# Fewer, larger transfers of V, wo and w_up, and reader-less matmuls placed anew, in a decode layer on one core

## The chip, the cores and the metric

The kernel runs on one core of a Trainium2 chip. The metric is the device time of one execution in microseconds; the time before is the median of three runs, 188.31 us (188.06 to 188.40).

## The reference

One decode step (one token, batch 2) of a transformer layer whose two halves are modulated by a condition c. Model width D = 640, 32 heads of width 192, the last W = 1024 rows of a cache of 4096, and a feed-forward part of width 1536. Everything is bfloat16. Cut to what matters:

```python
mod = (silu(c) @ w_mod).reshape(B, 6, 1, D)            # sa, ca, ga, sb, cb, gb
h = layernorm(x) * (1 + ca) + sa
q = (h @ wq) as [b, 32, 1, 192]
k, v = k_cache[:, :, -1024:], v_cache[:, :, -1024:]
o = softmax(q @ k.T * 192 ** -0.5) @ v                 # for each b and head
x = x + ga * (o as [b, 1, 6144] @ wo)
h = layernorm(x) * (1 + cb) + sb
out = x + gb * ((gelu(h @ w_gate) * (h @ w_up)) @ w_down)
```

## The kernel before

Each operation is appended to a list of its engine in program order, and the lists are emitted as they stand, with semaphore waits worked out from what each operation reads and writes. So every engine works strictly in the order in which the functions are called. All transfers are issued by SyncE, one after the other, through one queue; a transfer that has to wait for its buffer holds up those behind it on SyncE.

The stages are:

- The modulation w_mod and the projection wq are loaded, then the caches. A cache item is a transfer of one or two tiles. A tile is 64 positions of each partition (a head has four partitions), so that four tiles make up the window of one batch row. There are six places for tiles: four in `ring`, and two in `r1`, once wq is used up. `items` lists the transfers in order with their slot and their semaphore, and `load_kv(n)` issues them up to the n-th.
- Scores (`d_mul` L465, `p_reduce` L476, `d_rows` L483): VectorE multiplies half a tile of K with the query, TensorE sums it with 12 matmuls against an identity matrix, VectorE adds up the rest. The softmax of both batch rows follows.
- Weighted sum (`d_mask` L511, `p_pv` L523): for each tile VectorE spreads the weights over a mask and TensorE runs 32 matmuls over the tile of V, called PV here. `normalize` (L536, L540) and `p_sel` (L548, 8 matmuls each batch row) bring the heads together. Four copies and three VectorE transposes (L599, the tiles `oT`, 16 each) make the left operand of the projection.
- Projection wo (L630): 48 tiles, four matmuls of 32 columns each a tile, one TensorE operation for each transfer of wo, all in one accumulator. wo lies in `r1`, so that its transfers wait for the last PV of batch row 0.
- Second layer norm (a chain of VectorE operations, from L636 to the transpose L358), then `ffn_gu` (L648) for w_gate and w_up, 20 matmuls in all for each. Gelu on ScalarE (L655), product `geglu` (L662), transpose (L358), and the `down` projection (L671) of 12 tiles in three transfers. The product with the gate and the residual sum (L678, L680) and the store close the kernel. w_gate, w_up and w_down lie in slots of `ring`, and their transfers wait for the first two PV of batch row 1.

Between these stand matmuls without a reader: `warm(n, bk)` (L454) runs n matmuls of an identity matrix with the query into a PSUM bank that nobody reads, and `filler(n)` runs 4 n of them. They occupy TensorE for a while where it would stand idle.

```python
def filler(n=1):
    warm(n * ND, BK_W)          # ND = 4
```

Of the kernel before, what the change touches and what calls it, by code (L numbers as in the profile page):

```python
# [103 lines left out]
def bass_adaLN_cond__sliding_block_cached__geglu_ffn__decode_kernel(  # L104
# [49 lines left out]
    NS = 4  # L154
    SL = J * Dh
    WQ_SPLIT = [5]
    assert sum(WQ_SPLIT) == KT
    WO_SPLIT = [16, 16, 12, 4]
    OT_SPLIT = [16, 16, 16]
    assert sum(WO_SPLIT) == NT and sum(OT_SPLIT) == NT  # L160
    WU_SPLIT = [3, 2]
    assert sum(WU_SPLIT) == KT
    WD_SPLIT = [6, 4, 2]
    assert sum(WD_SPLIT) == FT
    ND = 4

    WO_WARM = [0, 8, 0, 9]
    WU_WARM = [3, 5]
    WD_WARM = [5, 0, 0]

    es = ExitStack()
    with es:
        S = _Sched(nc, es)
# [21 lines left out]
        def tile_f(slot, n=1):  # L195
            if slot < NS:
                return ring_f[:, slot * SL:(slot + n) * SL]
            return r1[:, (slot - NS) * SL:(slot - NS + n) * SL]
# [60 lines left out]
        def bank(k):  # L259
            return ("bank", k)  # L260
# [4 lines left out]
        sem_wq = [S.sem("d_wq%d" % i) for i in range(len(WQ_SPLIT))]  # L265
        sem_wo = [S.sem("d_wo%d" % i) for i in range(len(WO_SPLIT))]
        sem_wg = S.sem("d_wg")
        sem_wu = [S.sem("d_wu%d" % i) for i in range(len(WU_SPLIT))]
        sem_wd = [S.sem("d_wd%d" % i) for i in range(len(WD_SPLIT))]
        sem_ring = [S.sem("d_ring%d" % i) for i in range(4)]  # L270
        sem_out = S.sem("d_out")

        def k_dma(dst, src):
            return lambda e: e.dma_start(dst, src)  # L274
# [48 lines left out]
        def ring_keys(slot):  # L323
            return [half_key(slot, 0), half_key(slot, 1)]
# [9 lines left out]


        items = [("k", 0, 0, 2, 0, 0), ("k", 0, 2, 2, 2, 1), ("k", 1, 0, 2, NS, 2), ("k", 1, 2, 2, 0, 0), ("v", 0, 0, 2, 2, 1),
                 ("v", 0, 2, 2, NS, 2), ("v", 1, 0, 2, 0, 0), ("v", 1, 2, 1, 2, 1), ("v", 1, 3, 1, 3, 3)]
        place = {(kind, b, t0 + i): slot + i for kind, b, t0, nt, slot, _ in items for i in range(nt)}
        assert NTL == 4 and len(place) == 4 * NTL

# [3 lines left out]
        def load_kv(upto, deps=()):  # L344
            while keep["kv"] < upto:
                kind, b, t0, nt, slot, sm = items[keep["kv"]]
                cache = A_v_cache if kind == "v" else A_k_cache
                S.dma("sp", k_dma(tile_f(slot, nt),
                                  cache[b, :, K0:Sk, :].rearrange("h (q r) d -> h q r d", q=QP)[:, :, J * t0:J * (t0 + nt), :].rearrange("h q r d -> h q (r d)")),
                      sem_ring[sm], writes=[k for i in range(nt) for k in ring_keys(slot + i)], deps=deps, name="ld_%s%d_%d" % (kind, b, t0))  # L350
                keep["kv"] += 1
# [98 lines left out]
        def warm(n, bk):  # L450
            def f(e):
                last = None
                for _ in range(n):
                    last = e.matmul(ps[:, bk, 0:2 * Dh], lhsT=ident_b[:, :], rhs=qbc[:, :, :].rearrange("p b d -> p (b d)"),  # L454
                                    start=True, stop=True)
                return last
            if n:
                S.op("pe", f, reads=["ident_b", "qbc"], writes=[bank(bk)], name="warm")

        def filler(n=1):  # L460
            warm(n * ND, BK_W)
# [48 lines left out]
        def d_mask(b, t):  # L510
            S.op("dve", lambda e: e.tensor_tensor(out=Em[:, t % 2, :, :], in0=E_sb[:, b, J * t:J * (t + 1)].unsqueeze(2).broadcast_to([P, J, H]),  # L511
                                                  in1=M32b[:, :].unsqueeze(1).broadcast_to([P, J, H]), op=ALU.mult),
                 reads=[("E", b), "M32b"], writes=[("Em", t % 2)], name="mask%d_%d" % (b, t))

        def p_pv(b, t):
            vs = slot_of("v", b, t)
            n = J // 2

            def f(e):
                last = None  # L520
                for jp in range(n):
                    r = 2 * SQ * (jp % 2)
                    last = e.matmul(ps[r:r + 2 * H, BK_O, 0:ON],  # L523
                                    lhsT=Em[:, t % 2, 2 * jp:2 * jp + 2, :].rearrange("p j c -> p (j c)"),
                                    rhs=tile_v(vs)[:, 2 * jp:2 * jp + 2, :],
                                    start=(t == 0 and jp < 2), stop=(t == NTL - 1 and jp >= n - 2), tile_position=(0, r), skip_group_check=True)
                return last
            keep[("pv", b, t)] = S.op("pe", f, reads=[("Em", t % 2)] + ring_keys(vs), writes=[bank(BK_O)], name="PV%d_%d" % (b, t))
# [15 lines left out]
        def p_sel(b):  # L544
            def f(e):
                last = None
                for m in range(HM):
                    last = e.matmul(ps[:, BK_H + m // 2, (m % 2) * Dh:(m % 2 + 1) * Dh], lhsT=SEL[:, b, m, :], rhs=On[:, b, :],  # L548
                                    start=(b == 0 and m % 2 == 0), stop=(b == 1), skip_group_check=True)
                return last  # L550
            S.op("pe", f, reads=["SEL"] + [("On", b, g) for g in range(NJ)], writes=[bank(BK_H + c) for c in range(NQC)], name="sel%d" % b)
# [11 lines left out]
        def weighted(b, ta, tb):  # L563
            for t in range(ta, tb):
                d_mask(b, t)
                p_pv(b, t)
# [10 lines left out]
        softmax(0)  # L577
        softmax(1)
        weighted(0, 0, 2)
        load_kv(9)  # L580
        weighted(0, 2, 4)
        normalize(0)
        for t in range(NTL):
            d_mask(1, t)
            p_pv(1, t)
            if t < NTL - 1:
                filler((0, 3, 4)[t])
            else:
                p_sel(0)
        normalize(1)  # L590
        warm(3, 1)
        p_sel(1)
        warm(10, 1)
        assert keep["kv"] == len(items)
        for c in range(NQC):
            move(("act", "dve")[c % 2], oc[:, QC * c:QC * (c + 1)], ps[:, BK_H + c, 0:QC], [bank(BK_H + c)], [("oc", c)], "oc%d" % c)
# [6 lines left out]
        wo_src = A_wo.rearrange("(p t) n -> p t n", t=NT)  # L603
        wo_of = [(sum(WO_SPLIT[:i]), sum(WO_SPLIT[:i + 1])) for i in range(len(WO_SPLIT))]
        for i, (ta, tb) in enumerate(wo_of):
# [7 lines left out]
        k0 = 0  # L613
        for ci, nk in enumerate(WU_SPLIT):
            S.dma("sp", k_dma(wu_v[:, k0:k0 + nk, :].rearrange("p k n -> p (k n)"), wu_src[:, k0:k0 + nk, :].rearrange("p k n -> p (k n)")),
# [9 lines left out]
        for i, (ta, tb) in enumerate(wo_of):  # L625
# [7 lines left out]
            S.op("pe", f, reads=[("wo", i)] + [("oT", t) for t in range(ta, tb)], writes=[bank(BK_M)], name="wo%d" % i)  # L633
            warm(WO_WARM[i], 1)

# [7 lines left out]
        def ffn_gu(bk, wv, key, name, ka, kb):  # L643
            def f(e):
                last = None
                for k in range(ka, kb):
                    for j in range(NJ):
                        last = e.matmul(ps[SQ * j:SQ * j + SQ, bk, 0:FN], lhsT=hT[:, k, :], rhs=wv[:, k, FN * j:FN * j + FN],  # L648
                                        start=(k == 0), stop=(k == KT - 1), tile_position=(0, SQ * j), skip_group_check=True)
                return last  # L650
            S.op("pe", f, reads=["hT", key], writes=[bank(bk)], name="ffn_" + name)

        ffn_gu(BK_G[0], wg_v, "wg", "wg", 0, KT)
        warm(2, 1)
        S.op("act", lambda e: e.activation(out=gl, in_=ps[:, BK_G[0], 0:FN], func=ACTF.Gelu_apprx_tanh),  # L655
             reads=[bank(BK_G[0])], writes=["gl"], name="gelu")
        k0 = 0
        for ci, nk in enumerate(WU_SPLIT):
            ffn_gu(BK_G[1], wu_v, ("wu", ci), "wu%d" % ci, k0, k0 + nk)
            k0 += nk  # L660
            warm(WU_WARM[ci], 1)
        S.op("dve", lambda e: e.tensor_tensor(out=aC[:, :], in0=ps[:, BK_G[1], 0:FN], in1=gl, op=ALU.mult),  # L662
# [72 lines left out]
```

## Time and profile before

| what | before |
|---|---|
| time, median of 3 runs | 188.31 us (188.06 to 188.40) |
| time of the profiled execution | 188.0 us |
| its span, first to last instruction | 186.3 us |
| TensorE matmuls busy | 120.3 us (65%), 1043 instructions |
| TensorE weight loads busy | 61.7 us (33%), 1043 instructions |
| VectorE busy | 106.6 us (57%), 114 instructions |
| ScalarE busy | 13.9 us (7%) |
| read from HBM | 76.88 MB, 413 GB/s over the span |
| packets of the DMA engines | 3069 |

Times in the profile are microseconds from the start of the span. PE is TensorE's matmuls and PEld its weight loads, DVE is VectorE, ACT ScalarE, SP SyncE. Each matmul has a weight load of its own. A row of the timeline has the start, the duration, the engine, the line, the operation, the tiles (out, then in), the shapes and how many were merged into the row; in brackets stands the time that the engine was idle before, and what ended it. "issue" there means that no awaited semaphore shows. The DMA view lists queues with their packets, megabytes and the time that the packets took as a share of 16 engines over the window; queue q1 carries the kernel's transfers and q8 the program's instructions. A share over a short window counts all packets that begin in it at their full length, so it can be over 100%.

### The profile page before, as it was taken

What the parts mean: (1) busy time and instruction counts of PE and PEld (TensorE: products, weight loads), DVE (VectorE), ACT (ScalarE), POOL (GpSimd) and SP (SyncE); (2) the same over time, 40 slices, a digit from 0 to 9 for tenths busy, and PEclk for the clock granted to TensorE, in tenths of its full rate; (3) what the DMA queues carried; (4) which work ended last, traced back from release to release, by engine and by line L of the source; (5) the groups of instructions that cost most, each with busy time, mean ns of one, the idle gap of its engine ahead of it and who ended that gap; (6) DMA issues with size and microseconds to landing.
All of it is one profiled execution on the core that took longest, in us unless ns stands there. A gap on an engine that the chain in (4) does not pass through costs nothing.

```text
span 186.3 us, 2324 instructions
## 1 busy us (share of the span) xinstructions
PE 120.3 (65%) x1043; PEld 61.7 (33%) x1043; DVE 106.6 (57%) x114; ACT 13.9 (7%) x24; POOL 4.9 (3%) x12
## 2 busy tenths in 40 slices
PE   0004500871089999989999894449919999687763
PEld 0001200440034334334333332326605566354321
DVE  6801600020588999999999983294465800743431
ACT  2002400023000000000000000100010001500400
POOL 8200000000000000000000000000000000000000
PEclk9999999998559999999999999558996999999998
DMA  7999999898999989899998999999899999999990
GB/s 256 404 449 489 449 449 409 348 500 359 486 454 391 498 359 478 369 475 454 401 464 380 478 391 464 412 443 454 362 433 427 421 429 427 429 405 425 419 373 27
DMA packets 3069, 77.02 MB, mean 413 GB/s; under 512 B 372, under 2 KB 372, under 8 KB 1012
## 3 DMA queue, kind: packets, MB, share of 16 engines
q1 hardware_dynamic: 3060, 76.88, 96.5%
q8 instruction: 8, 0.13, 0.3%
q14 instruction: 1, 0.01, 0.0%
HBM read 76.88 MB, written 0.00 MB: 413 GB/s over the span
## 4 chain that ended last, share of the span: by engine, by line
DMA 41%; DVE 36%; PE 16%; SPq 3%; ACT 1%; issue 1%; POOL 0%; POOLq 0%; DVEq 0%
DMA ring<-in_A_k_cache_dram 24%; DVE ring L465 19%; DMA ring<-in_B_w_down_dram 17%; PE ps L523 10%; DVE r L465 7%; DVE Sg L483 5%; PE ps L476 4%; SPq L274 3%; DVE Em L511 2%; ACT E_sb L502 1%; PE ps L504 1%; PE ps L498 1%; DVE On L540 0%; ACT On L536 0%; PE ps L491 0%
## 5 line engine op out<-in xcount | busy, mean ns | idle before, releaser
L465 DVE TENSOR_TENSOR ring<-ring,qbc 128x6144 bf16<-128x6144 bf16 x12 | 40.1, 3349 | 8.5 <-DMA ring<-in_A_k_cache_dram 8.5
L476 PE MATMUL ps<-ring,ident_b 128*128 128x512 bf16 x144 | 34.7, 393 | 13.0 <-DVE ring L465 13.0
L454 PE MATMUL ps<-qbc,ident_b 128*128 128x384 bf16 x149 | 28.7, 326 | 0.7 <-ACT qbc L432 0.7
L476 PEld LDWEIGHTS ps<-ring,ident_b 128*128 128x128 bf16 x144 | 13.6, 100 | 32.7 <-DVE ring L465 17.2
L523 PE MATMUL ps<-ring,Em 128*64 128x384 bf16 x192 | 19.7, 371 | 6.6 <-DVE Em L511 6.6
L511 DVE TENSOR_TENSOR Em<-E_sb,M32b 128x2048 bf16<-128x2048 bf16 x8 | 18.1, 2289 | 5.5 <-PE ps L523 5.5
L454 PEld LDWEIGHTS ps<-qbc,ident_b 128*128 128x128 bf16 x149 | 13.8, 98 | 12.5 <-issue 2.4
L523 PEld LDWEIGHTS ps<-ring,Em 128*64 128x64 bf16 x192 | 12.0, 125 | 13.9 <-DVE Em L511 7.1
L401 PE MATMUL ps<-ring,scT 128*32 128x480 bf16 x40 | 4.4, 601 | 15.6 <-DVE scT L358 15.6
L465 DVE TENSOR_TENSOR r<-r,qbc 128x6144 bf16<-128x6144 bf16 x4 | 13.4, 3348 | 0.0
L424 PE MATMUL ps<-r,hT 128*32 128x384 bf16 x80 | 5.9, 480 | 11.0 <-DMA r<-in_A_wq_dram 11.0
L483 DVE TENSOR_REDUCE Sg<-ps 128x32 f32<-128x512 f32 x16 | 11.0, 685 | 3.4 <-PE ps L476 3.4
L476 PE MATMUL ps<-r,ident_b 128*128 128x512 bf16 x48 | 11.1, 380 | 1.8 <-DVE r L465 1.8
L434 DVE CAST aux<-ps 128x384 bf16<-128x384 f32 x4 | 2.0, 553 | 16.9 <-PE ps L424 16.0
L540 DVE TENSOR_SCALAR On<-ps,rden 32x192 bf16<-32x192 f32 x4 | 1.7, 418 | 12.6 <-ACT On L536 12.6
L424 PEld LDWEIGHTS ps<-r,hT 128*32 128x32 bf16 x80 | 3.2, 137 | 14.1 <-issue 11.8
L476 PEld LDWEIGHTS ps<-r,ident_b 128*128 128x128 bf16 x48 | 4.4, 98 | 8.1 <-DVE r L465 3.4
L401 PEld LDWEIGHTS ps<-ring,scT 128*32 128x32 bf16 x40 | 1.2, 132 | 17.1 <-DVE scT L358 15.6
L502 ACT ACTIVATE E_sb<-Sg,nb 128x256 bf16<-128x256 f32 x2 | 1.0, 508 | 75.6 <-DVE nb L501 75.6
L630 PE MATMUL ps<-r,aux 128*32 128x160 bf16 x192 | 4.1, 233 | 3.0 <-issue 1.2
L523 PE MATMUL ps<-r,Em 128*64 128x384 bf16 x64 | 5.4, 327 | 0.0
L630 PEld LDWEIGHTS ps<-r,aux 128*32 128x32 bf16 x192 | 3.4, 96 | 4.1 <-issue 3.1
(73 smaller groups left out, 65.7 us busy)
## 6 DMA issues: line engine op xcount, KB each, us to landing
ring<-in_A_k_cache_dram SPq DMA_DIRECT2D x3, 6144.0 KB, 40.7
ring<-in_A_v_cache_dram SPq DMA_DIRECT2D x2, 6144.0 KB, 23.3
r<-in_A_wq_dram SPq DMA_DIRECT2D x1, 7680.0 KB, 30.5
r<-in_A_k_cache_dram SPq DMA_DIRECT2D x1, 6144.0 KB, 38.5
r<-in_A_v_cache_dram SPq DMA_DIRECT2D x1, 6144.0 KB, 23.2
ring<-in_A_v_cache_dram SPq DMA_DIRECT2D x2, 3072.0 KB, 17.6
r<-in_A_wo_dram SPq DMA_DIRECT2D x2, 2560.0 KB, 23.7
ring<-in_w_mod_dram SPq DMA_DIRECT2D x1, 4800.0 KB, 14.2
```

Of the source, the lines that this page charges most:

```text
L274: return lambda e: e.dma_start(dst, src)
L401: last = e.matmul(ps[SQ * j:SQ * j + SQ, bk, 0:3 * DN].rearrange("p (i n) -> p i n", i=3), lhsT=scT[:, k, :], rhs=wm_v[:, k, 3 * part * D: ...
L424: last = e.matmul(ps[SQ * j:SQ * j + SQ, BK_H + c, 0:QC], lhsT=hT[:, k, :], rhs=wq_v[:, k, RN * j + QC * c:RN * j + QC * (c + 1)], start=( ...
L434: S.op("dve", lambda e: e.tensor_copy(out=dst, in_=src), reads=reads, writes=writes, name=name)
L454: last = e.matmul(ps[:, bk, 0:2 * Dh], lhsT=ident_b[:, :], rhs=qbc[:, :, :].rearrange("p b d -> p (b d)"), start=True, stop=True)
L465: S.op("dve", lambda e: e.tensor_tensor(out=tile_v(ks)[:, hf * JH:(hf + 1) * JH, :], in0=tile_v(ks)[:, hf * JH:(hf + 1) * JH, :], in1=qbc[ ...
L476: last = e.matmul(o_ap, lhsT=ident_b[:, :], rhs=tile_v(ks)[:, hf * JH:(hf + 1) * JH, ci * GC:(ci + 1) * GC], start=(ci == 0), stop=(ci == ...
L483: S.op("dve", lambda e: e.tensor_reduce(out=S_sb[:, b, a:a + JH], in_=ps[:, hf, 0:JH * GC].rearrange("p (j c) -> p j c", j=JH), axis=AX.X, ...
L502: S.op("act", lambda e: e.activation(out=E_sb[:, b, :], in_=S_sb[:, b, :], func=ACTF.Exp, scale=SCALE, bias=nb[:, 0:1], accum_out=esum[:, ...
L511: S.op("dve", lambda e: e.tensor_tensor(out=Em[:, t % 2, :, :], in0=E_sb[:, b, J * t:J * (t + 1)].unsqueeze(2).broadcast_to([P, J, H]), in ...
L523: last = e.matmul(ps[r:r + 2 * H, BK_O, 0:ON], lhsT=Em[:, t % 2, 2 * jp:2 * jp + 2, :].rearrange("p j c -> p (j c)"), rhs=tile_v(vs)[:, 2 ...
L630: last = e.matmul(ps[SQ * j:SQ * j + SQ, BK_M, 0:DN], lhsT=oT[:, t, :], rhs=wo_v[:, t, DN * j:DN * j + DN], start=(t == 0), stop=(t == NT ...
```

## The change

The last two tiles of V come in one transfer (one item and one semaphore fewer). wo comes in two transfers of 36 and 12 tiles, where there were four of 16, 16, 12 and 4, and its matmuls are in two operations instead of four. w_up comes in one transfer, with its 20 matmuls in one operation. The reader-less matmuls move: between the PV of batch row 1 there were 12 after the second and 16 after the third, and there are now 16 after the second and none after the third; ahead of wo there were 10 and are 26; behind the operations of wo there were 0, 8, 0 and 9 and are 8 and 9; behind w_gate there were 2 and are 14; behind those of w_up there were 3 and 5 and are 5. The bytes and the other arithmetic are the same.

```diff
-    WO_SPLIT = [16, 16, 12, 4]
+    WO_SPLIT = [36, 12]
...
-    WU_SPLIT = [3, 2]
+    WU_SPLIT = [5]
...
-    WO_WARM = [0, 8, 0, 9]
-    WU_WARM = [3, 5]
+    WO_WARM = [8, 9]
+    WU_WARM = [5]
...
-        sem_ring = [S.sem("d_ring%d" % i) for i in range(4)]
+        sem_ring = [S.sem("d_ring%d" % i) for i in range(3)]
...
-                 ("v", 0, 2, 2, NS, 2), ("v", 1, 0, 2, 0, 0), ("v", 1, 2, 1, 2, 1), ("v", 1, 3, 1, 3, 3)]
+                 ("v", 0, 2, 2, NS, 2), ("v", 1, 0, 2, 0, 0), ("v", 1, 2, 2, 2, 1)]
...
-        load_kv(9)
+        load_kv(8)
...
             if t < NTL - 1:
-                filler((0, 3, 4)[t])
+                filler((0, 4, 0)[t])
             else:
                 p_sel(0)
         normalize(1)
         warm(3, 1)
         p_sel(1)
-        warm(10, 1)
+        warm(26, 1)
...
         ffn_gu(BK_G[0], wg_v, "wg", "wg", 0, KT)
-        warm(2, 1)
+        warm(14, 1)
```

## The prediction

> **What bounds the kernel now.** I read the page first, then TensorE's timeline of the last 30 us, then the DMA view over short windows. From the page:
>
> ```profile
> DMA  7999999898999989899998999999899999999990
> ...
> q1 hardware_dynamic: 3060, 76.88, 96.5%
> q8 instruction: 8, 0.13, 0.3%
> ```
>
> The transfers' packets fill 96.5% of 16 DMA engines, and what is missing lies before the first packets (about 3 us) and after the last landing (the chain of waits has the final w_down part landing at 183.05 us, 3.2 us before the span's end at 186.3). So bytes set the end, and all work beside them is free, as long as the compute after the last landing is short: 8 matmuls at 183.10, then the closing VectorE operation L678 at 183.47.
>
> TensorE's timeline (start, duration, what, in brackets the idle time before it and who ended it):
>
> ```profile
> 149.04 2.79 PE L523 MATMUL ps<-ring,Em 128*64 128x384 bf16 x32
> 151.77 2.77 PE L454 MATMUL ps<-qbc,ident_b 128*128 128x384 bf16 x16
> 154.47 2.79 PE L523 MATMUL ps<-ring,Em 128*64 128x384 bf16 x32
> ...
> 159.79 1.79 PE L454 MATMUL ps<-qbc,ident_b 128*128 128x384 bf16 x10
> 162.73 2.62 PE L630 MATMUL ps<-r,aux 128*32 128x160 bf16 x128 [1.14 <-DVE aux L599]
> 165.28 1.47 PE L454 MATMUL ps<-qbc,ident_b 128*128 128x384 bf16 x8
> 167.39 0.25 PE L630 MATMUL ps<-r,aux 128*32 128x160 bf16 x3 [0.63 <-DMA r<-in_A_wo_dram]
> 168.86 1.28 PE L630 MATMUL ps<-r,aux 128*32 128x160 bf16 x61 [1.23 <-issue]
> ...
> 174.76 1.00 PE L648 MATMUL ps<-ring,hT 128*32 128x384 bf16 x20 [0.61 <-DVE hT L358]
> ...
> 183.10 0.32 PE L671 MATMUL ps<-ring,aux 128*32 128x160 bf16 x8 [0.32 <-DMA ring<-in_B_w_down_dram]
> ```
>
> The row to stop at is 168.86. The third wo part has 48 matmuls and waited for its data until 167.39, yet only 3 ran; then TensorE stood 1.23 us on "issue", which no data or semaphore explains. The DMA view tells what happened there. Its rows are queue, packets, MB, share; the windows are 107 to 118, 137 to 147, 162.7 to 166.39, 166.39 to 166.41, 72.10 to 72.12 and 102.92 to 102.94 us:
>
> ```profile
> q1 hardware_dynamic: 96, 4.72, 99.2%
> ...
> q1 hardware_dynamic: 192, 4.33, 100.8%
> ...
> q1 hardware_dynamic: 153, 1.56, 99.8%
> ...
> q8 instruction: 1, 0.02, 320.6%
> ...
> q8 instruction: 1, 0.02, 332.5%
> ...
> q8 instruction: 1, 0.02, 343.1%
> ```
>
> An instruction packet began at 166.40; it took 320.6% x 16 x 0.02 = 1.03 us, and TensorE resumed 1.44 us after its end. I read the stall as TensorE having run out of program. The interval fits: the packets at 72.11 and 102.94 lie eight rounds of 12 + 4 matmuls apart, 128 matmuls, each with its weight load. Count 128 back from the stall: 3 of the third wo part, 8 reader-less, 64 and 53 of the first two parts. So the earlier boundary is 11 matmuls into the first wo part, at 162.95. There the next block was asked for; no instruction packet is in the window 162.7 to 166.39, it came at 166.40, and the program went on at 168.86: **5.9 us from the asking**.
>
> **The change part by part.**
>
> *Packets.* The windows 107 to 118 and 137 to 147 hold packets of 48 KB and 24 KB: 99.2% x 16 x 11 / 96 = 1.819 us, and 100.8% x 16 x 10 / 176 = 0.916 us (16 of the 192 are semaphore writes). Two small ones less one large one: 0.012 us. Each transfer puts 8 packets on each engine, so four fewer save 4 x 8 x 0.012 = 0.39 us. That shortens the DMA path: last landing 182.66. The page "DMA: Bandwidth & Descriptors" of the Trainium skill (section "Anatomy of one DMA — SWDGE (gpsimd) path") gives a transfer of that path a fixed cost of about 2.0 us; were it so here and exposed, four would be worth 8 us, but packets that fill 99 to 101% of the engines leave no such gap here.
>
> *SyncE.* It issues four transfers fewer and waits as before; the merged V transfer is issued at 130.59, when its second slot comes free, where the first half went at 128.03. The transfer ahead of it works until 135.86 (issued 113.52, 22.3 to landing), so DMA has 5.3 us of cover. Without the cover the loss would be 2.55 us. No cost.
>
> *V.* The merged pair lands at 150.69 (issued 130.59, 20.1 to landing) less 0.1, so the third PV waits from 149.8 to 150.6 instead of starting at 149.04; then 64 matmuls go without the 16 reader-less ones between (5.4 us, row at 130.41). PV ends at 156.0, before at 157.26: 1.25 us earlier. The transposes oT (161.12 to 165.25) end at 164.0. The 26 reader-less matmuls (from 158.5, 0.164 each) end at 162.8, hidden.
>
> *wo in 36 and 12.* 36 tiles land when the two 16s did (issued 136.21, 26.5 to landing: 162.7) plus a third of the 12-tile part behind them (landing 4.6 us later, 1.5), less 0.15: 164.1. The first part needs all three transposes now. It starts at 164.15.
>
> *The block boundary.* Ahead of wo the program has 12 reader-less matmuls fewer (28 to 16) and 16 more (10 to 26), so 4 more: the boundary that stood 11 matmuls into wo now stands 7 in, and the next one 135 in, of 144. TensorE gets there at 164.15 + 135 x 0.0205 = 166.9 (128 took 2.62). The 8 reader-less matmuls and the wait until 167.39 that lay between are gone: before, the block had 4.5 us (162.95 to 167.45), now 2.75. How long does it take? From below, the packets at 72.11 and 102.94 began within 0.1 us of the boundary's matmul: 0.1 + 1.03 + 1.44 = 2.6 us, no stall. From above, behind all of the second wo part on an engine (8 packets of 0.58 = 4.6): 7.1 us. I take the 5.9 of the same operation behind the same 15 KB packets. TensorE resumes at 164.3 + 5.9 = **170.2**.
>
> The page "Runtime: NRT & Kernel Launch" (section "Instruction fetch mechanics") speaks against this: it calls the crossing of a block boundary mostly hidden. The 1.23 us before 168.86 is not. By the page the sum would be the 0.39 us gain alone, 187.9.
>
> *From there to the end*, by the rows: 9 matmuls of wo 0.2; 8 reader-less 1.4 (next start after them); 48 of wo 1.05 (61 took 1.32 to the next VectorE start): second layer norm starts at 172.85, before at 170.18. Norm to first w_gate matmul 4.6 (174.76): 177.45. w_gate 0.93; 14 reader-less 2.4 (12 took 2.05): 180.75, when w_up has long landed (147.94 + 30.5 = 178.4 before). All 20 w_up matmuls to the geglu product 1.1 (8 took 0.63, 12 more at 0.04); geglu and transpose 1.5; down 0.55, 5 reader-less 0.92, last 24 down matmuls 0.7: L678 starts at **185.5**, before at 183.47. So 2.05 us later.
>
> Without a stall wo ends at 167.1, the second part lands at 168.6, the norm starts at 169.65, L678 could start at 182.3 and is held by the landing: 182.66 + 0.42 = 183.08. The 8, the 14 and all of w_up after one landing are then covered by transfers, and w_up in one costs 0.5 us of cover. With the stall that cover is gone: the 4.3 us of the 8, the 14 and the longer w_up all lie on the path.
>
> The profiled execution took 188.0 us, 1.7 more than its span; 188.0 + 2.05 = 190.05. The median of the runs is 188.31, 0.3 above it, so I predict **190.3**.
>
> **Rivals.**
>
> *The landing sets the end, and it is faster*: 187.9 (188.31 - 0.39). One mechanism: the block comes early. It decides when TensorE can go on before 167.7, which leaves 182.66 the later end: 3.6 us from wo's start. For it: fetches in the scores stage began within 0.1 us. Against: the one in this operation took 5.9.
>
> *A block in between*, resuming at 167.7 to 168.5: within 0.38 us of now, 187.9 to 188.6. No row of this stage lies there.
>
> *The stall also takes the clock*: after TensorE's idle 135.84 to 139.98 the granted clock was 0.50 from 140.57 to 143.98, and PV matmuls took double. The new idle time, 3.3 us, is a little shorter. Half clock over the 8 reader-less and the second wo part adds about 1.5 us: 191.8.
>
> *DMA runs dry behind the merged V*: needs more than 5.3 us from issue to first packet; I give it nothing of its own.
>
> **How the numbers follow.** Stall at full clock 0.60 (forecast, 190.3; its own range is 188.8 to 191.5, by a block time of 4.4 to 7.1 us). Stall at half clock 0.17. In between 0.07. Landing sets the end 0.16. Faster or slower counts from 0.2%, about what a measurement of this kernel can tell from no change: faster 0.16, same 0.07, slower 0.77. For 8 in 10 the range reaches down over the in-between case to the landing's 187.9 and up to the clock case: 187.8 to 191.6.
>
> **What would show it.** Right: an "issue" gap of some 3 us in the middle of the first wo operation, about 135 matmuls in, an instruction packet starting 3 us after wo starts, the wo part's last matmuls near 170, the norm near 172.9, w_up waiting for nothing, and the last down matmuls waiting for TensorE's own order instead of a landing; last landing near 182.7. Wrong: 144 wo matmuls in one piece, and L671 still waiting for w_down. Wrong in size: the gap differs, or the clock shows 0.50 after 167.

## The result, and the profile after

The changed kernel took 192.58 us (median of six executions, 189.81 to 194.15), the kernel before, beside it, 188.21 us (six, 188.06 to 188.99). The ratio is 1.0137 (95% interval 1.0097 to 1.0178): slower by 1.4%. It leaves out the three longest executions, the profiled one among them, as slow ones; the medians of all six stand 2.3% apart. The control below shows the same gap, the same clock and the same times (four executions, 191.26 to 193.87 us).

The executions fall in two groups by the mean granted TensorE clock: 189.81 and 190.18 us at 0.936 and 0.937, and 192.42 to 194.15 us at 0.928 and 0.929.

The page of the profiled execution (194.15 us, span 192.4): clock in tenths, DMA busy in tenths, and the transfers' queue.

```profile
PEclk9999999998559999999999997569978999996999
DMA  7999998998998998999989989989999899999700
...
q1 hardware_dynamic: 2484, 76.88, 93.5%
```

There are 576 packets fewer, and DMA is done two slices before the end, where before it was busy to the last slice but one. So the landings no longer set the end; the last w_down part lands at 150.05 + 34.8 = 184.85 us, and the closing L678 starts at 189.59. The clock drops once more, to 0.6 in slice 37 (173 to 178 us).

TensorE's timeline after:

```profile
148.09 2.77 PE L454 MATMUL ps<-qbc,ident_b 128*128 128x384 bf16 x16
153.07 5.39 PE L523 MATMUL ps<-ring,Em 128*64 128x384 bf16 x64 [2.21 <-DMA ring<-in_A_v_cache_dram]
...
160.99 4.39 PE L454 MATMUL ps<-qbc,ident_b 128*128 128x384 bf16 x26
166.58 2.53 PE L630 MATMUL ps<-r,aux 128*32 128x160 bf16 x136 [1.21 <-DVE aux L599]
172.69 0.32 PE L630 MATMUL ps<-r,aux 128*32 128x160 bf16 x8 [3.57 <-issue]
172.94 2.74 PE L454 MATMUL ps<-qbc,ident_b 128*128 128x384 bf16 x8
175.62 1.32 PE L630 MATMUL ps<-r,aux 128*32 128x160 bf16 x48
...
181.57 1.00 PE L648 MATMUL ps<-ring,hT 128*32 128x384 bf16 x20 [0.60 <-DVE hT L358]
182.50 2.45 PE L454 MATMUL ps<-qbc,ident_b 128*128 128x384 bf16 x14
184.88 1.00 PE L648 MATMUL ps<-ring,hT 128*32 128x384 bf16 x20
...
188.94 0.60 PE L671 MATMUL ps<-ring,aux 128*32 128x160 bf16 x24
```

Three things are to be seen. The first wo operation is cut: 136 matmuls, 3.57 us on "issue", then its last 8. From there on TensorE never waits for a transfer: w_up, w_down and the second wo part follow in TensorE's own order. And the third PV waits for V until 153.07, where 150.6 was expected.

The DMA view, first over 166.6 to 170.19 us, then 170.19 to 170.21:

```profile
q1 hardware_dynamic: 114, 1.52, 99.1%
...
q8 instruction: 1, 0.02, 288.1%
```

The program's packet came 3.6 us after wo had begun, took 288.1% x 16 x 0.02 = 0.92 us, and TensorE went on 1.57 us after its end: 6.1 us from wo's start. TensorE by windows (length, PE busy, PEld, DVE, ACT, POOL, granted clock, DMA share, GB/s), the gap and what followed it:

```profile
168.88:172.69 3.81, 0.24 (x17) 0.08 (x5) 0.00 (x0) 0.00 (x0) 0.00 (x0) 1.00 0.98 411
172.92:176.33 3.41, 3.41 (x39) 1.75 (x36) 0.00 (x0) 0.00 (x0) 0.00 (x0) 0.50 1.00 424
```

After the gap the clock was 0.50 for 3.4 us: the 8 reader-less matmuls took 2.68 us to the next operation (172.94 to 175.62), where at full clock they take 1.40 (167.63 to 169.03 in the run with V alone below).

### The profile page after: what moved, and what is told of

It reads as the page before. It is cut to its first block, busy times and chain, and to the rows that moved or that the text cites. A ratio compares the mean times of both kernels' runs of the same rounds, so it can differ in the third digit from the quotient of the medians.

```text
span 192.4 us, 2343 instructions
## 1 busy us (share of the span) xinstructions
PE 123.1 (64%) x1056; PEld 64.6 (34%) x1056; DVE 106.5 (55%) x114; ACT 13.9 (7%) x24; POOL 4.9 (3%) x12
## 4 chain that ended last, share of the span: by engine, by line
DVE 39%; DMA 35%; PE 20%; issue 3%; ACT 1%; SPq 0%; POOL 0%; POOLq 0%; DVEq 0%
DMA ring<-in_A_k_cache_dram 24%; DVE ring L465 19%; DMA ring<-in_A_v_cache_dram 11%; DVE r L465 7%; PE ps L523 7%; DVE Sg L483 5%; PE ps L476 4%; PE ps L454 3%; PE ps L630 2%; DVE aux L599 2%; DVE Em L511 1%; PE ps L648 1%; ACT E_sb L502 1%; PE ps L671 1%; DVE aux L434 1%
## 5 line engine op out<-in xcount | busy, mean ns | idle before, releaser
L476 PE MATMUL ps<-ring,ident_b 128*128 128x512 bf16 x144 | 35.5, 399 | 14.0 <-DVE ring L465 14.0
L454 PE MATMUL ps<-qbc,ident_b 128*128 128x384 bf16 x162 | 31.7, 336 | 0.7 <-ACT qbc L432 0.7
L454 PEld LDWEIGHTS ps<-qbc,ident_b 128*128 128x128 bf16 x162 | 15.6, 101 | 13.8 <-issue 3.1
L523 PEld LDWEIGHTS ps<-ring,Em 128*64 128x64 bf16 x192 | 13.1, 127 | 15.5 <-DVE Em L511 7.1
L424 PE MATMUL ps<-r,hT 128*32 128x384 bf16 x80 | 5.0, 426 | 11.0 <-DMA r<-in_A_wq_dram 11.0
L401 PEld LDWEIGHTS ps<-ring,scT 128*32 128x32 bf16 x40 | 1.2, 132 | 16.9 <-DVE scT L358 15.5
## 6 DMA issues: line engine op xcount, KB each, us to landing
r<-in_A_wo_dram SPq DMA_DIRECT2D x1, 1920.0 KB, 33.7
```

The lines of the kernel that those rows point to most:

```text
L401: last = e.matmul(ps[SQ * j:SQ * j + SQ, bk, 0:3 * DN].rearrange("p (i n) -> p i n", i=3), lhsT=scT[:, k, :], rhs=wm_v[:, k, 3 * part * D: ...
L424: last = e.matmul(ps[SQ * j:SQ * j + SQ, BK_H + c, 0:QC], lhsT=hT[:, k, :], rhs=wq_v[:, k, RN * j + QC * c:RN * j + QC * (c + 1)], start=( ...
L476: last = e.matmul(o_ap, lhsT=ident_b[:, :], rhs=tile_v(ks)[:, hf * JH:(hf + 1) * JH, ci * GC:(ci + 1) * GC], start=(ci == 0), stop=(ci == ...
L523: last = e.matmul(ps[r:r + 2 * H, BK_O, 0:ON], lhsT=Em[:, t % 2, 2 * jp:2 * jp + 2, :].rearrange("p j c -> p (j c)"), rhs=tile_v(vs)[:, 2 ...
```

## Experiments

Three theories. *Program block*: the gap is TensorE waiting for the next block of its program, asked for when wo began, too late for a wo without pauses. *Operations*: two long wo operations, and the reader-less matmuls between, are the cost by themselves. *Transfer*: the merged V lands late and pushes the rest. Ratios are to the kernel before, run beside it on the same chip, where it took 187.9 to 188.1 us; the median behind each ratio is of the run's executions, and the ratio is not the quotient of medians.

**32 matmuls more ahead of wo.**

```diff
 # scores(), changed kernel
-                    filler()
+                    warm(ND + 2, BK_W)
```

> The changed kernel with two more reader-less matmuls in each of the 16 rounds of the scores stage (32 more ahead of wo; each round has some 0.45 us of idle TensorE for the 0.33 us they take). Program-block theory (the 3.6 us gap in the first wo operation is TensorE waiting for the next block of its program, asked for when wo began): the boundary now lies about 24 matmuls ahead of wo, the block is asked for some 4 us earlier, no gap inside wo, its 144 matmuls in one piece, and the time falls to 187.9 to 188.5 us. Operations theory (two long wo operations, with 8 and 14 reader-less matmuls on the way, are what costs): unchanged, 190 to 194 us. Transfer theory (the merged V lands late, at 152.9 us instead of 150.7, on one DMA engine): the gap may go, but the last landing stays near 184.9 us and the time near 189.8 us.

Ratio 1.0045 (1.0010 to 1.0079), 188.54 us, ten executions from 187.66 to 190.21. TensorE's timeline:

```profile
164.32 2.67 PE L630 MATMUL ps<-r,aux 128*32 128x160 bf16 x144 [1.24 <-DMA r<-in_A_wo_dram]
166.93 1.48 PE L454 MATMUL ps<-qbc,ident_b 128*128 128x384 bf16 x8
168.92 1.01 PE L630 MATMUL ps<-r,aux 128*32 128x160 bf16 x48 [0.52 <-DMA r<-in_A_wo_dram]
```

All 144 matmuls in one piece, and the second part waits for its data. The instruction packet is at 162.10 us, ahead of wo. L678 starts at 183.13, with the last landing at 148.97 + 33.7 = 182.7. The operations are those of the changed kernel, so they are not the cost by themselves. The spread up to 190.21 is left over.

**Four matmuls more, as a control.**

```diff
 # scores(), changed kernel
-                    filler()
+                    warm(ND + (1 if (b, t) in ((0, 2), (1, 2)) else 0), BK_W)
```

> The changed kernel with four more reader-less matmuls in the scores stage, one in each of four rounds. A control for the run with 32: hardly any time is added. Program-block theory: the gap stays as long (3 to 4 us) but moves four matmuls up, to after about the 132nd of wo's first operation instead of the 136th; the time stays at 190 to 194 us. Operations theory: the same time, and the gap at the 136th matmul, since it would belong to the operation and not to the count. If mere extra work in the scores stage were what helps, this run would be faster than the changed kernel.

Ratio 1.025 (1.020 to 1.030), 192.75 us (191.26 to 193.87). TensorE's timeline:

```profile
164.46 2.47 PE L630 MATMUL ps<-r,aux 128*32 128x160 bf16 x132 [1.24 <-DMA r<-in_A_wo_dram]
171.19 0.39 PE L630 MATMUL ps<-r,aux 128*32 128x160 bf16 x12 [4.26 <-issue]
```

The gap moved from the 136th to the 132nd matmul, by the four that were put in some 60 us earlier or more. That ties it to the count of the program and to nothing in wo. The instruction packet came at 168.89. Here V landed at 130.83 + 19.9 = 150.7, as expected in the prediction, and still the time is 192.75; the clock was 0.50 after the gap (over 171.55 to 174.90).

**wo alone, in the kernel before.**

```diff
-    WO_SPLIT = [16, 16, 12, 4]
-    WO_WARM = [0, 8, 0, 9]
+    WO_SPLIT = [36, 12]
+    WO_WARM = [8, 9]
```

> The kernel before with wo alone changed: 36 and 12 tiles, 8 and 9 reader-less matmuls behind them. Program-block theory: the boundary stays 11 matmuls into wo, the next is 139 in, of 144; the gap of about 3 us stands there; the second norm starts near 172.8 us and the time is 189.0 to 189.6 us at full clock, about 1 us above before (some 1.5 us more where the clock falls to half). Transfer theory: V is as before, so the time is that of before, 188.0 us. Operations theory: between, up to 189 us, without a gap.

Ratio 1.0246 (1.0216 to 1.0276), 192.41 us (190.80 to 192.91): 2.8 us above the expectation at full clock, 1.3 above it with half clock.

```profile
160.87 1.79 PE L454 MATMUL ps<-qbc,ident_b 128*128 128x384 bf16 x10
166.47 3.99 PE L630 MATMUL ps<-r,aux 128*32 128x160 bf16 x140 [3.81 <-DVE aux L599]
172.28 0.25 PE L630 MATMUL ps<-r,aux 128*32 128x160 bf16 x4 [1.81 <-issue]
```

The gap stands at the 140th matmul (139 expected). But with 10 reader-less matmuls ahead instead of 26, TensorE stood 3.81 us ahead of wo, the clock was 0.50 from 166.0 to 169.4, and wo itself ran more slowly: 140 matmuls in 3.99 us, where the changed kernel took 2.53 for 136. wo also began at 166.47, 3.7 us later than before: it now waits for all three transposes, and in this execution the scores stage was already 0.9 us late. That the 26 of the change are worth something where wo comes in two parts is read from this idle time; no run changes them alone.

**V alone, in the kernel before.**

```diff
-                 ("v", 0, 2, 2, NS, 2), ("v", 1, 0, 2, 0, 0), ("v", 1, 2, 1, 2, 1), ("v", 1, 3, 1, 3, 3)]
+                 ("v", 0, 2, 2, NS, 2), ("v", 1, 0, 2, 0, 0), ("v", 1, 2, 2, 2, 1)]
...
-        load_kv(9)
+        load_kv(8)
```

> The kernel before with V alone changed: its last two tiles in one transfer. Program-block theory: the boundary stays where it was (11 matmuls into wo, the gap of 1.2 us behind the third wo part's wait), so 188.1 us, 0.1 less than before. Transfer theory: the pair lands near 152.9 us in some or all executions, every landing behind it is 1.5 to 2 us late, and the time is 189.5 to 190 us.

Ratio 1.0057 (1.0025 to 1.0089), 189.06 us (188.40 to 189.99): 1.1 us that the prediction put at nothing. In its profile the pair was issued at 132.02 and landed at 151.2, and the chain that ended last runs from there over TensorE: the 16 reader-less matmuls, which this run keeps behind the third PV, wo, and an "issue" gap in it that has grown to 2.07 us, from 1.23 before.

**The merged V held back further.**

```diff
 # on the run with 32 more
-        load_kv(8)
-        weighted(0, 2, 4)
+        weighted(0, 2, 3)
+        load_kv(8, deps=[keep["pv", 0, 2]])
+        weighted(0, 3, 4)
```

> The run with 32 more matmuls (no gap in wo), with the merged V transfer held back until the third PV of batch row 0 as well, so issued at about 133.3 us instead of 130.7. If the merged V transfer arrives late because it is issued too close to the end of the transfer ahead (all its engines have begun their last packet by 133.6), this adds most of the 2.6 us: V lands at 152.5 to 153.5 us, the last landing is near 185 us and the time 189.8 to 190.8 us, in every execution. If the 5.3 us of cover of the prediction were real, nothing changes: 187.7 us.

Ratio 1.0098 (1.0065 to 1.0130), 189.88 us (189.33 to 190.50), and no execution near 187.7. The issue is at 134.93; the DMA view over 132 to 134.93, 134.93 to 136.2, and 136.2 to 136.6:

```profile
q1 hardware_dynamic: 22, 0.49, 39.1%
...
q1 hardware_dynamic: 4, 0.00, 0.2%
...
q1 hardware_dynamic: 15, 0.74, 570.3%
```

DMA runs dry from before the issue, and the first data packets start 1.3 us after it. V lands at 134.93 + 18.6 = 153.5. So the time between the issue and the end of the transfer ahead does count.

**wo in four parts again, the rest of the change kept.**

```diff
-    WO_SPLIT = [36, 12]
-    WO_WARM = [8, 9]
+    WO_SPLIT = [16, 16, 12, 4]
+    WO_WARM = [0, 8, 0, 9]
```

> The changed kernel with wo in its four parts again (16, 16, 12, 4, and 0, 8, 0, 9 reader-less matmuls behind them); V and w_up merged, the other reader-less matmuls as in the changed kernel. Program-block theory: the boundary still lies about 7 matmuls into wo, but 8 reader-less matmuls and the wait for the third part lie inside the block again, so the gap is 1 to 2.5 us, near the third part's wait; the time is that of V alone merged, 188.2 to 189.9 us, not 192.6. Operations theory in the form that the 14 and 26 moved matmuls cost: still 190 us or more. Transfer theory: as V alone, 188.4 to 190 us.

Ratio 1.0031 (1.0000 to 1.0063), 188.20 us (187.74 to 190.35). There was no "issue" gap at all:

```profile
162.99 2.40 PE L630 MATMUL ps<-r,aux 128*32 128x160 bf16 x128
165.32 1.47 PE L454 MATMUL ps<-qbc,ident_b 128*128 128x384 bf16 x8
167.57 1.01 PE L630 MATMUL ps<-r,aux 128*32 128x160 bf16 x48 [0.78 <-DMA r<-in_A_wo_dram]
```

My 1 to 2.5 us were too much: the third part's 48 matmuls start when its data come. The pauses that four parts leave were enough here, but the packet was early too. It came at 165.10, 2.1 us after wo had begun, where the changed kernel's took 3.6. Where it came later, four parts did not hide it: 1.23 us of gap in the kernel before, 2.07 with V alone, 2.05 with w_up alone.

**Fewer reader-less matmuls, the gap kept.**

```diff
 # changed kernel
-    WO_WARM = [8, 9]
+    WO_WARM = [0, 9]
...
         ffn_gu(BK_G[0], wg_v, "wg", "wg", 0, KT)
-        warm(14, 1)
+        warm(2, 1)
```

> The changed kernel without the 8 reader-less matmuls behind the first wo operation and with 2 instead of 14 behind w_gate. Program-block theory: the gap of 3 to 4.5 us in wo stays, but the work behind it is shorter by 1.4 us (2.7 us at half clock) and 2.0 us, so the time falls from 192.6 to 188.5 to 190 us. Operations theory: the same fall, or more, since these would be the whole of the loss (188 us). The gap in the first wo operation tells them apart.

Ratio 1.0052 (1.0025 to 1.0080), 188.91 us (188.08 to 190.12).

```profile
165.47 2.54 PE L630 MATMUL ps<-r,aux 128*32 128x160 bf16 x136 [1.27 <-DMA r<-in_A_wo_dram]
171.51 1.15 PE L630 MATMUL ps<-r,aux 128*32 128x160 bf16 x56 [3.51 <-issue]
```

The gap is as long as in the changed kernel, yet most of the loss is gone, and the end follows the last landing again (150.35 + 33.5 = 183.85, then L678 at 184.25). So the gap costs only as far as the work behind it reaches past the landings. Two things made that work shorter, and this run does not part them: the 20 reader-less matmuls are gone, 3.4 us at full clock, and no half clock followed the gap.

**32 more, and V in two transfers.**

```diff
 # on the run with 32 more: items, load_kv and sem_ring of the kernel before
```

> The run with 32 more matmuls (no gap in wo), with V's last two tiles in two transfers again. Both costs of the change are then gone: the program's block is asked for early, and V is issued with its old cover. 187.5 to 187.9 us in every execution, 0.1 to 0.3 us below before by three transfers fewer (3 x 8 x 0.012 = 0.29 us), without the spread to 190.2 us. If the spread of the run with 32 more (187.7 to 190.2) did not come from V, it stays.

Ratio 0.9989 (0.9973 to 1.0004), 187.95 us, twelve executions from 187.62 to 188.22, seven of them above the 187.9 that was expected of all. The spread to 190 is gone with the merged V. Not faster than before by more than the measurement can tell. In its profile (188.22 us) wo ran at half clock:

```profile
164.37 4.32 PE L630 MATMUL ps<-r,aux 128*32 128x160 bf16 x144 [2.16 <-DMA r<-in_A_wo_dram]
```

The clock was 0.50 from 164.94 to 168.35, after TensorE had been idle for only 2.16 us.

**The same with fewer reader-less matmuls.**

```diff
 # on the run above
-    WO_WARM = [8, 9]
+    WO_WARM = [0, 9]
...
-        warm(14, 1)
+        warm(2, 1)
```

> The run with 32 more matmuls and V in two transfers, without the 8 reader-less matmuls behind the first wo operation and with 2 instead of 14 behind w_gate. In that run the executions at 187.9 to 188.2 us had wo at half clock and then 1.4 + 2.0 us of reader-less matmuls on the way to the end. If both costs are as the program-block and transfer theories say, nothing but the landings is left: 187.5 to 187.8 us in nearly every execution, 0.1 to 0.25% below before. If the reader-less matmuls were needed to keep the clock up, it is slower: 188.5 us or more.

Ratio 1.0000 (0.9988 to 1.0012), 188.14 us. The expected 0.1 to 0.25% did not come. The fastest executions are 187.66 us here, 187.62 in the run above and 187.79 of the kernel before beside this run: at most the size that was expected, and lost in the spread.

**w_up alone, in the kernel before.**

```diff
-    WU_SPLIT = [3, 2]
-    WU_WARM = [3, 5]
+    WU_SPLIT = [5]
+    WU_WARM = [5]
...
-        warm(2, 1)
+        warm(14, 1)
```

> The kernel before with w_up alone in one transfer, and its reader-less matmuls (14 behind w_gate, 5 behind w_up). Ahead of and in wo nothing changes. All theories: within 0.2% of before, 187.8 to 188.2 us: one transfer fewer is worth 0.1 us, and the 12 more w_up matmuls behind the landing (0.5 us) and the 14 reader-less ones stay inside the cover that the last landings give. If w_up in one were itself a cost, 188.5 us or more.

Ratio 1.0017 (0.9995 to 1.0039), 188.24 us: no change that can be told. Its executions reach 190.02, which I did not follow up.

No version ran clearly faster than the kernel before.

## Why the prediction was right, and where not

*Direction and cause: right.* The gap was forecast after about 135 matmuls of the first wo operation, and stood after 136, with the instruction packet 3.6 us after wo's start (3 forecast), and TensorE going on 6.1 us after wo's start (6.05 forecast: 164.15 to 170.2). In the control it was 6.7 us. That the cause is the program's block and not the operation is shown by the two shifts: four matmuls put in far ahead move the gap by four, 32 take it away.

*The work behind the gap: right at full clock.* From TensorE's going on to L678 the sum gave 15.3 us. Measured: 189.59 - 172.69 = 16.9, and 17.0 in the control. The 1.6 us more are the half clock: the 8 reader-less matmuls 2.68 instead of 1.4, the second wo part 1.37 instead of 1.05 until the norm starts.

*The number: right for a minority of the executions.* In the profiled one L678 starts at 189.59, 4.1 us after the forecast 185.5: 2.4 because wo began at 166.58 instead of 164.15, behind a late V, 0.1 by the block, 1.6 by the clock. The two executions at the higher clock, 189.81 and 190.18 us, fit the forecast of 190.3; they have no profile, so that they ran as forecast is not shown. The median of all six, 192.58, lies above the whole range, which ended at 191.6, because the range took a half clock and a longer block each by itself. In the control they came together, with V in time: wo began 0.3 us later than forecast, the block took 0.7 more and the work behind it 1.7 more, and that execution took 192.73.

*The clock: the price was right, the chance not.* The rival priced half clock at 1.5 us more and got 0.17; it cost 1.6, and four of six executions have the lower mean clock. The step that failed is the comparison of the new idle time, "3.3 us", with the 4.1 us before ("a little shorter"), because the length of the gap alone does not decide. Gaps of 3.57 and 4.26 us were followed by half clock, one of 3.51 us (fewer reader-less matmuls) was not, and one of 2.16 us (32 more, V in two) was. In these traces the granted clock changes only at steps of 3.41 us (in the kernel before it stayed for 6.83, 10.24, 61.44, 10.24, 13.65, 3.41 and 40.96 us). It fell to half where TensorE had been idle for 61% or more of the step before, and not at 54% or less, in all twelve traces from 110 us on. In the changed kernel the step from 169.47 to 172.89 was idle for 94%, in the run with the gap of 2.16 us the step ahead of wo's half clock for 63%. The gap of 3.51 us lay across two steps, idle for 50% and 52%, and the clock stayed. So the place of a gap on these steps decides together with its length.

*The merged V: wrong.* The prediction gave SyncE's later issue "5.3 us of cover" and "No cost", and its rival nothing. V alone cost 0.57%, 1.1 us. Two terms of the sum were mis-sized. The cover was counted to the landing of the transfer ahead, which is its last engine; on the first engines its last packets end at about 133.6, when the window 133.6 to 135.3 begins to fill with the next transfer's. And the issue is not where the transfer starts: in the run with V held back 1.3 us passed before data moved. From 130.59 that leaves 133.6 - 130.6 - 1.3 = 1.7 us. In three profiles the issue comes later, at 131.74 to 132.02 us, and 0.3 to 0.6 us are left. That delay is not made by the merged V. In these three the first 12 matmuls of the scores stage took 5.0 to 5.3 us instead of 4.3, more of them at half clock, and all that follows is late; the runs with wo alone and with fewer reader-less matmuls and V in two have the same delay, and the latter still took 187.87 us. As far as these profiles show, the merged V only takes away the room that absorbed it.

The pairs of issue and landing: 130.73 and 150.6, 130.83 and 150.7, 131.74 and 152.9, 132.02 and 151.2, 132.02 and 151.7, held back 134.93 and 153.5. The three late landings do not follow the order of issue, so the cover does not explain their size. DMA did not stand idle there as it did with V held back: from 133.4 to 136 the changed kernel's 42 packets took 136.7% of the window, where 42 took 115.7% in the run with 32 more, whose V was in time. The packets took longer; why is open. That the spread up to 190 us of single executions comes from the merged V follows from the run with V in two transfers, which lost it; in which executions it happens was seen only in these profiles.

*Packets: not settled.* The last landing was forecast at 182.66, from 183.05 before. It is 182.7 in the run with 32 more and 182.6 with V in two, but 183.2 with wo in four parts, which still has two transfers fewer than before. One profile of each cannot show 0.39 us, and no ratio does.

*w_up in one: right as far as can be told.* Its cost stayed inside the cover (ratio 1.0017, interval across 1).

Taken together: without the wo merge the change costs 0.3% (1.0031), without the block boundary 0.45% (1.0045), with both present 1.4% (2.5% in the control). The wo merge costs by taking away pauses in which a block could arrive; with the block early the same two transfers cost little or nothing (0.9989 with V in two).

The page "Runtime: NRT & Kernel Launch" of the Trainium skill (section "Instruction fetch mechanics") calls the boundary's cost mostly hidden. In these runs it is hidden in the scores stage and with 32 matmuls more; it is not where 256 instructions run in under 3 us, as wo's do here (132 to 136 matmuls in 2.5 us, each with its weight load).

## What to carry to other kernels

Look for gaps on "issue" in the middle of one operation, and for an instruction packet inside them: a stretch of short matmuls without pauses can outrun the supply of the program, and a few matmuls more or fewer, far ahead, decide whether it does. A wait for data that looks like waste may be what hides it. Count the cover of a later transfer from its first data packet, not from its issue, to the end of the transfer ahead on its first engine, not to the landing; even this smaller count did not account for all of the delay here. And reader-less matmuls that fill a wait become part of the path as soon as something ahead of them is late.

## What the runs showed that I had not expected

The program's packet came late in wo, and not by a fixed time: counted from wo's start, 2.1 us with wo in four parts, 3.6 in the changed kernel, 3.8 and 4.4 in the runs with fewer reader-less matmuls and with four more, while in the scores stage it came at once. What it waits for was not tried. And the gap on TensorE from 169.12 to 172.69 was followed by half clock from 172.89 to 176.30, so that the price of a stall can lie behind the stall.
